# Where a fused kernel's weight conversions stand, and when its P tiles are loaded

## The chip, the core and the metric

The kernel runs on one core of a Trainium2 chip. The time is that of the device, in microseconds (us), from one launch to its end; three runs of the kernel before had a median of 1813.38 us (1813.12 to 1814.7). The engines are PE (TensorE, matmuls), PEld (its weight loads), DVE (VectorE), ACT (ScalarE), POOL (GpSimd) and SP (SyncE, which here issues every DMA in the order of the program).

## The reference, cut to what matters

```python
a = exp(phi - max(phi, axis=2)); a = a / (sum(a, axis=2) + 1e-09)          # 8 batches, 8 heads, 576 x 32
k_m = einsum('bhsm,bhsd->bhmd', a, k); v_m = einsum('bhsm,bhsd->bhmd', a, v)
attn = softmax(scale * q @ k_m.T)                                          # over 32 memory slots
x = (attn @ v_m), heads side by side: 4608 tokens x 512
h = x @ w_in;  x = (h - tanh(h)) @ w_out                                   # first layer, 512 -> 2048 -> 512
h = x @ w3;    out = where(h > 0, h, exp(min(h, 0)) - 1) @ w4              # second layer, the same sizes
```

The four weight matrices arrive as 64-bit floats. A value is used as a pair of words, high part and rest, and each product of pairs takes three matmuls.

## The kernel before, in words

**First layer.** The product `attn @ v_m @ w_in` is regrouped: `v_m @ w_in` (`vw_half`, L304, tile `vw_ps`, kept as `vw`) is made once for a pair of batches, and the softmax rows P (tile `p`, written to `p_dram` by the attention and loaded by `load_p`, L291) are multiplied with it (`h_unit`, L319, tile `h_ps`). The feed-forward width of 2048 is cut in four, the tokens in 16 tiles of 288, which makes 64 *blocks* (`bi` 0 to 63). A block is two *halves* (`i` 0 and 1), and a half does, in this order: one `h_unit`; the elementwise function of it (`g_a` to `g_d`: ACT L330 to L333, POOL L338, DVE L339, then DVE L344 and L345, and in the next half ACT L351 and POOL L352, tile `g`); two `x_unit` (L364, tile `x_ps`, the product with `w_out`), of which ACT copies the first (L371) and, after block 22, DVE the second (L373). `x_unit`, `vw_half` and parts of the attention share three PSUM buffers (`misc`). Every fourth block (3, 7, ..., 59) also makes the next group's `vw`, two `vw_half` in each of its halves; this is called a *border* below.

**Work on the side.** Two `Staged` queues of generators advance by one step each time `round()` is called: `units` with the 16 attention units (blocks 0 to 22; in each, DVE L120 makes a row maximum `cmax`, which PE transposes in the next round, L123), and `cv` with the weight conversions. A conversion of 128 x 512 weights loads `raw` (one of three buffers), waits some rounds, and then does one stage a round: ACT L48 (`abs`, into the one PSUM buffer `cv_m`), DVE L50 and L51, DVE L54 and L55 (which read `cv_m` for the last time and write `cv_a`), ACT L58, POOL L60. First-layer weights stay in SBUF; second-layer weights are staged in `wst` and stored to `w_dram` (L541). `cv` advances once a half, twice in blocks 0 to 6 and 28 and 29, and starts a conversion every second round. `need(kind, pg)` calls `round()` at once, as often as it takes until these weights are there, and `open_l2` at block 60 calls `drain()`, which does so until nothing is left; it then opens the second layer's pools where the first one's buffers were.

**Second layer.** From the end of block 63 on, PE goes through 18 token tiles of 256 with matmuls L420 and L457. Blocks 60 to 63 already load its first activations (`xr`, L393, summed by DVE L402) and weights.

Of the kernel before, what the change touches and what calls it, by code (L numbers as in the profile page):

```python
# [62 lines left out]
class Attention:  # L63
# [44 lines left out]
    def unit(self, u, nxt, eng, first_p=None):  # L108

        nc, wk, sm = self.nc, self.wk, self.sm  # L110
        b, g = divmod(u, 2)
# [8 lines left out]
        nc.vector.tensor_reduce(cmax, ph.rearrange("p h c m -> p h m c"), axis=AX.X, op=ALU.max)  # L120
        yield
        mT = ps_tile([128, 96], "mT")
        nc.tensor.transpose(mT, cmax.rearrange("p h m -> p (h m)"), ident[:96, :96])  # L123
# [116 lines left out]
class Staged:  # L240


    def __init__(self, gens=(), every=1):
        self.todo, self.live, self.every, self.wait = deque(gens), [], every, 0
        self.timed, self.rounds = deque(), 0
        self.first = deque()

    def at(self, rnd, gen):
        self.timed.append((rnd, gen))

    def round(self):
        while self.timed and self.timed[0][0] <= self.rounds:
            self.live.append(self.timed.popleft()[1])
        self.rounds += 1
        if self.wait > 0:
            self.wait -= 1
        if self.wait <= 0 and (self.first or self.todo):
            self.live.append((self.first or self.todo).popleft())
            self.wait = self.every
        for g in list(self.live):  # L260
            try:
                next(g)
            except StopIteration:
                self.live.remove(g)
# [6 lines left out]
class Moe1:  # L271


    def __init__(self, tc, ctx, const, p_dram, x2_dram):
        self.tc, self.nc, self.const = tc, tc.nc, const
        self.p_dram, self.x2_dram = p_dram, x2_dram
        pool = lambda name, n, **kw: ctx.enter_context(tc.tile_pool(name=name, bufs=n, reuse_waits="tile", **kw))
        self.x_p = pool("x2", 3)
        self.g_p = pool("g", 5)
        self.gw, self.gw1 = pool("gw", 3), pool("gw1", 1)  # L280
        self.p_p = pool("p", 2)
        self.vw_p = pool("vw", 1)
        self.vw, self.p, self.g, self.x2, self.work, self.x2_pool = {}, {}, {}, {}, {}, {}
# [195 lines left out]
def moe_kernel(tc, q, k, v, phi, w1, w2, w3, w4, out):  # L479
    nc = tc.nc  # L480
    with ExitStack() as top, tc.manual_schedule():
# [11 lines left out]
        m1 = Moe1(tc, l1a, const, p_dram, x2_dram)  # L493
# [18 lines left out]
        def conv(layer, kind, pg, c, lead=2):  # L512
# [6 lines left out]
            else:  # L519
                r0 = 256 * pg + 128 * c  # L520
                nc.sync.dma_start(out=raw, in_=w[r0:r0 + 128, :])
            for _ in range(lead + 1):
                yield
            staged = []
# [19 lines left out]
        conv_l1 = lambda kind, *pgs: [g for pg in pgs for g in conv_pair(1, kind, pg)]  # L544
# [15 lines left out]
        cv = Staged([conv(1, "i", 1, 1)] + conv_l1("o", 0, 1), 2)  # L560
        cv.wait = 4
        for k, g in enumerate(cv_first):
# [54 lines left out]
        def store_late():  # L617
            while late:
                m1.store_x(*late.pop(0))
# [49 lines left out]

        soon = deque()  # L670
        for bi, (ss, bp, sub, j) in enumerate(blocks):
# [28 lines left out]
            if at1_open and 2 * B - 1 in p_done:  # L700
# [3 lines left out]
                cv.first.extend(conv_l1("o", 4, 5))  # L704
            if bi == 18:
                cv.todo.extend(conv_l2)
            if bi == 24:
                cv.first.extend(conv_l1("i", 4, 5))
            if bi == 28:
# [3 lines left out]
            if nxt and nxt not in m1.p:  # L713
                m1.load_p(*nxt)
            for i in range(2):
                pg = 2 * sw + i
                m1.h_unit(sw, n, pg)
                m1.g_a(n, pg)
                m1.g_b(n, pg)
                store_late()  # L720
                if soon:
# [15 lines left out]
                m1.g_c(n, pg)  # L737
                if bi < 7 or 28 <= bi < 30:
                    cv.round()
                units.round()  # L740
                if vw_next:
# [59 lines left out]
```

## Time and profile before

| | |
|---|---|
| median of three runs | 1813.38 us |
| the profiled execution | 1815.06 us, span 1813.3 us, 1.8 us around it |
| PE busy | 1624.8 us, 90% of the span |
| PE busy, 0 to 100 us | 42.5 of 100 us |
| PE busy, 100 to 950 us | 729.5 of 850 us (sum over windows of 50 us) |
| DVE, ACT, POOL busy | 1215.8, 960.8, 755.3 us |
| mean granted TensorE clock | 0.956 of full speed |

The span has three stretches: the start with the first attention units (to about 72 us, where the first `h_unit` stands), the 64 blocks of the first layer (to 986 us), and the second layer, in which PE has no idle time to speak of. A time in a row is counted from the first instruction of the span. The end of the idle time before a row stands in brackets with what released it.

### The profile page before, as it was taken

Reading aid. Unit: us, or ns where it says so; the run is one execution under the profiler, and the core shown is the slowest. Engines: PE = TensorE matmul, PEld = TensorE weight load, DVE = VectorE, ACT = ScalarE, POOL = GpSimd, SP = SyncE. Lnnn points to the kernel's source line nnn. Section 1 sums busy time; section 2 is a strip of 40 time slices with the busy share of each in tenths; the row PEclk is TensorE's granted clock in tenths of the full one; section 3 lists DMA queues with packets and bytes.
Section 4 is the critical chain, followed back from the end, with each engine's and each line's share of the span. In section 5 each row is a group of like instructions: output and inputs, shape, how many; then the busy total and the mean of one; then the engine's idle time right before and its main releaser. Section 6 shows DMA issues by size and latency. Waiting matters only on the chain.

```text
span 1813.3 us, 30112 instructions
## 1 busy us (share of the span) xinstructions
PE 1624.8 (90%) x11496; PEld 1496.5 (83%) x11496; DVE 1215.8 (67%) x1805; ACT 960.8 (53%) x1713; POOL 755.3 (42%) x539
## 2 busy tenths in 40 slices
PE   4467879888888989999949999999999999999998
PEld 2356778888887989999949999999999999999997
DVE  6868777677877888788855555555555555555554
ACT  3456767677877878787845333333333333333332
POOL 3245645555655656665634222222222222222222
PEclk7678999899998989999979999999999999999999
DMA  9466565675545456666657721221221221211110
GB/s 241 133 165 177 150 185 171 168 200 165 191 163 167 155 165 196 204 198 200 199 163 263 300 59 59 59 59 59 59 59 59 59 59 59 59 59 59 59 35 24
DMA packets 140935, 238.40 MB, mean 131 GB/s; under 512 B 8184, under 2 KB 102392, under 8 KB 138744
## 3 DMA queue, kind: packets, MB, share of 16 engines
q1 hardware_dynamic: 140792, 236.49, 42.9%
q8 instruction: 91, 1.49, 0.4%
q14 instruction: 52, 0.43, 0.1%
HBM read 159.78 MB, written 75.50 MB: 130 GB/s over the span
## 4 chain that ended last, share of the span: by engine, by line
PE 68%; DVE 11%; ACT 7%; DMA 7%; issue 4%; POOL 2%; SPq 0%; DVEq 0%; ACTq 0%; POOLq 0%
PE h_ps L420 23%; PE o_ps L457 22%; PE x_ps L364 14%; PE h_ps L319 7%; DMA p<-p_dram 5%; DVE vw L309 2%; ACT vw L307 1%; DVE cv_a L55 1%; DVE cv_m L54 1%; DVE h_ps L339 1%; ACT t L330 1%; PE vw_ps L304 1%; ACT g L351 1%; DVE s L344 1%; ACT u L331 1%
## 5 line engine op out<-in xcount | busy, mean ns | idle before, releaser
L364 PE MATMUL x_ps<-g,w 128*128 128x288 f32 x3072 | 466.2, 305 | 69.0 <-DVE vw L309 27.9
L364 PEld LDWEIGHTS x_ps<-g,w 128*128 128x128 f32 x3072 | 433.6, 195 | 84.5 <-issue 23.9
L420 PEld LDWEIGHTS h_ps<-x,wi 128*128 128x128 f32 x3456 | 429.7, 190 | 11.7
L420 PE MATMUL h_ps<-x,wi 128*128 128x256 f32 x3456 | 433.2, 281 | 0.0
L446 POOL TENSOR_TENSOR e<-hm,e 128x512 fp32r<-128x512 f32 x144 | 186.9, 1298 | 588.1 <-ACT e L445 443.8
L457 PE MATMUL o_ps<-wo,e 128*128 128x512 f32 x1728 | 423.8, 394 | 0.7 <-POOL e L446 0.7
L457 PEld LDWEIGHTS o_ps<-wo,e 128*128 128x128 f32 x1728 | 314.8, 188 | 65.0 <-POOL e L446 1.1
L431 ACT ACTIVATE t_ps<-hm 128x512 f32<-128x512 f32 x144 | 86.7, 602 | 515.2 <-DVE hm L430 515.2
L338 POOL TENSOR_TENSOR v<-t,u 128x576 f32<-128x576 f32 x128 | 183.5, 1433 | 215.7 <-ACT u L331 153.9
L319 PE MATMUL h_ps<-p,vw 128*128 128x288 f32 x1536 | 242.5, 310 | 23.8 <-DMA p<-p_dram 21.4
L352 POOL TENSOR_TENSOR g<-s,g 128x576 fp32r<-128x576 f32 x128 | 191.7, 1498 | 146.1 <-ACT g L351 130.7
L319 PEld LDWEIGHTS h_ps<-p,vw 128*128 128x128 f32 x1536 | 223.6, 200 | 27.6 <-issue 15.4
L437 DVE SCALAR_TENSOR_TENSOR hm<-hm,t_ps 128x512 f32<-128x512 f32 x144 | 99.1, 688 | 200.5 <-ACT hm L432 200.5
L430 DVE TENSOR_SCALAR hm<-h_ps 128x512 f32<-128x512 f32 x144 | 99.6, 692 | 140.0 <-PE h_ps L420 140.0
L339 DVE TENSOR_TENSOR h_ps<-h_ps,t 128x576 f32<-128x576 f32 x128 | 98.0, 766 | 82.4 <-ACT u L331 80.8
L330 ACT ACTIVATE t<-h_ps 128x576 f32<-128x576 f32 x128 | 83.2, 650 | 96.9 <-issue 44.4
L309 DVE TENSOR_TENSOR vw<-vw_ps,vw 64x512 fp32r<-64x512 f32 x128 | 88.1, 689 | 66.7 <-ACT vw L307 64.7
L344 DVE SCALAR_TENSOR_TENSOR s<-s,v 128x576 f32<-128x576 f32 x128 | 114.4, 894 | 4.0 <-POOL v L338 3.9
L345 DVE COPY_PREDICATED s<-big,h_ps 128x576 f32<-128x576 uint32 x128 | 106.6, 833 | 10.7
L333 ACT ACTIVATE big<-u,bias 128x576 f32<-128x576 f32 x128 | 97.9, 765 | 10.9 <-DVE s L345 10.9
L439 DVE TENSOR_TENSOR hm<-hm,h_ps 128x512 f32<-128x512 f32 x144 | 98.9, 687 | 5.0
L438 DVE SCALAR_TENSOR_TENSOR hm<-hm,t_ps 128x512 f32<-128x512 f32 x144 | 98.9, 687 | 4.9
(86 smaller groups left out, 1744.2 us busy)
## 6 DMA issues: line engine op xcount, KB each, us to landing
x_dram<-x SPq DMA_DIRECT2D x128, 288.0 KB
xr<-x_dram SPq DMA_DIRECT2D x72, 512.0 KB
p<-p_dram SPq DMA_DIRECT2D x62, 576.0 KB
raw<-in_moe_w_in_dram SPq DMA_DIRECT2D x32, 512.0 KB
raw<-in_moe_w_out_dram SPq DMA_DIRECT2D x32, 512.0 KB
w_dram<-wst SPq DMA_DIRECT2D x32, 512.0 KB
kv<-in_k_dram SPq DMA_DIRECT2D x16, 576.0 KB
kv<-in_v_dram SPq DMA_DIRECT2D x16, 576.0 KB
```

Source lines behind the costliest of these rows:

```text
L309: nc.vector.tensor_tensor(lo, src, r32(hi), op=ALU.subtract)
L319: nc.tensor.matmul(ps[:, j, :NB], lhsT=vw[a][:, kc, 128 * j:128 * j + 128], rhs=p[:, kc, b, :], start=(k == 0), stop=(k == 5))
L330: nc.scalar.activation(t, w[0], ACTF.Tanh)
L338: nc.gpsimd.tensor_tensor(v, t, u, op=ALU.mult)
L339: nc.vector.tensor_tensor(h, h, t, op=ALU.subtract)
L344: nc.vector.scalar_tensor_tensor(s, s, G_B, v, op0=ALU.add, op1=ALU.mult)
L345: nc.vector.copy_predicated(s, big.bitcast(U32), d)
L352: nc.gpsimd.tensor_tensor(g[:, 1], s, r32(g[:, 0]), op=ALU.subtract)
L364: nc.tensor.matmul(ps, lhsT=wo[pg][:, a, j, 128 * dm:128 * dm + 128], rhs=g[:, b, j, :], start=(k == 0), stop=(k == 11))
L420: nc.tensor.matmul(ps[:, j], lhsT=w3[:, a, kc, 128 * j:128 * j + 128], rhs=x[:, b, kc, :], start=(k == 0), stop=(k == 11))
L446: nc.gpsimd.tensor_tensor(e[:, 1], hm, r32(e[:, 0]), op=ALU.subtract)
L457: nc.tensor.matmul(self.acc[n][tg], lhsT=e[:, a, j, 128 * tg:128 * tg + 128], rhs=w4[:, b, j, :], start=(pg == 0 and j == 0 and i == 0), s ...
```

## The change

It alters the first layer alone: when steps of the side queues are issued, and two pool sizes. No operation is added or removed in the computation.

- `Staged` gets a list `apart` and a method `half()`. A conversion's last yield before its `abs` is true, which puts it on that list, so that its next step (`abs`) is issued at the next `half()`: after `g_c` in the same half of a block, and not at the next `round()`.
- `cv` advances twice a half in blocks 26 to 29 (before 28 and 29). The second-layer conversions are queued at block 14 (before 18), and those of `w_in` parts 4 and 5 are put ahead of `w_out` parts 4 and 5.
- The pool of `p` has three buffers (before two), that of `g` four (before five). `load_p` for block `bi + 2` is issued in block `bi` after the second `h_unit`, if the attention units that it needs were done before this block; otherwise one block ahead at its top, as before.
- An attention unit from the fifth on waits one more round between `cmax` and its transposition; the first start of `cv.todo` is one round later.

```diff
@@ Attention.unit
         yield
+        if u >= 4:
+            yield
         mT = ps_tile([128, 96], "mT")
@@ Staged
-        self.first = deque()
+        self.first, self.apart = deque(), []
     def round(self):
+        self.half()
...
-        for g in list(self.live):
+        self.step([g for g in self.live if g not in self.apart])
+
+    def half(self):
+
+        gens, self.apart = self.apart, []
+        self.step(gens)
+
+    def step(self, gens):
+        for g in gens:
             try:
-                next(g)
+                if next(g):
+                    self.apart.append(g)
@@ Moe1
-        self.g_p = pool("g", 5)
+        self.g_p = pool("g", 4)
-        self.p_p = pool("p", 2)
+        self.p_p = pool("p", 3)
@@ conv
-            for _ in range(lead + 1):
-                yield
+            for k in range(lead + 1):
+                yield k == lead
@@ the blocks
-        cv.wait = 4
+        cv.wait = 5
-            if bi == 18:
+            if bi == 14:
                 cv.todo.extend(conv_l2)
             if bi == 24:
-                cv.first.extend(conv_l1("i", 4, 5))
+                cv.first.extendleft(reversed(conv_l1("i", 4, 5)))
...
+            p_there |= p_done
...
+                if i == 1 and bi + 2 < len(blocks):
+                    ass, abp, asub, aj = blocks[bi + 2]
+                    far = (2 * ass + asub, 4 * abp + aj)
+                    if all(u in p_there for u in range(2 * (far[1] // 2) + 2)):
+                        m1.load_p(*far)
...
                 m1.g_c(n, pg)
-                if bi < 7 or 28 <= bi < 30:
+                cv.half()
+                if bi < 7 or 26 <= bi < 30:
                     cv.round()
+                    cv.half()
```

The line numbers grow by up to 20 with it (L48 to L60 stay; L307 is L319 afterwards, L330 is L342, L371 is L383, L120 stays, L291 is L303, L379 is L391, L393 is L405, L541 is L553).

**At a border.** These are ACT's instructions in the two halves of border block 51, from the first half's `vw` copies on. Before:

```order
L307 ACTIVATE vw<-vw_ps 64x512 x4
L330 ACTIVATE t<-h_ps 128x576
L331 ACTIVATE u<-h_ps 128x576
L332 ACTIVATE s<-u,bias 128x576
L333 ACTIVATE big<-u,bias 128x576
L371 ACTIVATE x<-x_ps 128x288
L48 ACTIVATE cv_m<-raw 128x512
L351 ACTIVATE g<-s 128x576
L307 ACTIVATE vw<-vw_ps 64x512 x4
```

Now:

```order
L319 ACTIVATE vw<-vw_ps 64x512 x2
L48 ACTIVATE cv_m<-raw 128x512
L319 ACTIVATE vw<-vw_ps 64x512 x2
L342 ACTIVATE t<-h_ps 128x576
L343 ACTIVATE u<-h_ps 128x576
L344 ACTIVATE s<-u,bias 128x576
L345 ACTIVATE big<-u,bias 128x576
L383 ACTIVATE x<-x_ps 128x288
L58 ACTIVATE wst<-cv_a 128x512
L363 ACTIVATE g<-s 128x576
L319 ACTIVATE vw<-vw_ps 64x512 x4
```

The `abs` (L48) has moved from between the second half's copy of `x_ps` and its `vw` to the first half, between the two pairs of `vw` copies; L58, which before stood ahead of the first half's `vw`, stands where L48 stood.

**At block 60.** DVE between the last `vw` of border block 59 and the first sum of the second layer's activations. Before, of 16 rows of conversions in a row the first eight:

```order
L309 TENSOR_TENSOR vw<-vw_ps,vw 64x512 x2
L50 TENSOR_SCALAR cv_m<-cv_m 128x512
L51 TENSOR_SCALAR cv_m<-cv_m 128x512
L54 SCALAR_TENSOR_TENSOR cv_m<-raw,cv_m 128x512
L55 SCALAR_TENSOR_TENSOR cv_a<-raw,cv_m 128x512
L50 TENSOR_SCALAR cv_m<-cv_m 128x512
L51 TENSOR_SCALAR cv_m<-cv_m 128x512
L54 SCALAR_TENSOR_TENSOR cv_m<-raw,cv_m 128x512
L55 SCALAR_TENSOR_TENSOR cv_a<-raw,cv_m 128x512
```

Now:

```order
L321 TENSOR_TENSOR vw<-vw_ps,vw 64x512 x2
L351 TENSOR_TENSOR h_ps<-h_ps,t 128x2x288
L385 COPY x<-x_ps 128x288
L356 SCALAR_TENSOR_TENSOR s<-s,v 128x576
L357 COPY_PREDICATED s<-big,h_ps 128x576
L351 TENSOR_TENSOR h_ps<-h_ps,t 128x2x288
```

No DVE step of a conversion is left there; what `drain()` still issues is one POOL L60 and its store.

**SP's queue in the same place**, from a store of weights on. Before:

```order
L541 DMA w_dram<-wst 256x1x512 x4
L291 DMA p<-p_dram 128x1x1152
L379 DMA x_dram<-x 128x2x288
L393 DMA xr<-x_dram 128x4x256
L379 DMA x_dram<-x 128x2x288
L393 DMA xr<-x_dram 128x4x256
L291 DMA p<-p_dram 128x1x1152
L379 DMA x_dram<-x 128x2x288
L393 DMA xr<-x_dram 128x4x256 x2
L379 DMA x_dram<-x 128x2x288
```

Now:

```order
L553 DMA w_dram<-wst 256x1x512 x2
L391 DMA x_dram<-x 128x2x288
L405 DMA xr<-x_dram 128x4x256
L303 DMA p<-p_dram 128x1x1152
L391 DMA x_dram<-x 128x2x288
L405 DMA xr<-x_dram 128x4x256
L391 DMA x_dram<-x 128x2x288
L405 DMA xr<-x_dram 128x4x256 x2
L303 DMA p<-p_dram 128x1x1152
L391 DMA x_dram<-x 128x2x288
```

Of the loads of `p`, that of block 61 now stands before the stores; the one of block 62 stands behind one `xr` load, and that of block 63 behind all four.

## Rows read from the trace of the kernel before

**Rows 1.** Timeline of PE, steady blocks to a border: start, us, instruction [idle before]

```profile
711.80 1.77 PE L319 MATMUL h_ps<-p,vw 128*128 128x288 f32 x12
716.60 1.77 PE L319 MATMUL h_ps<-p,vw 128*128 128x288 f32 x12
722.82 1.78 PE L319 MATMUL h_ps<-p,vw 128*128 128x288 f32 x12
730.63 1.77 PE L319 MATMUL h_ps<-p,vw 128*128 128x288 f32 x12
...
739.29 1.78 PE L319 MATMUL h_ps<-p,vw 128*128 128x288 f32 x12
```

**Rows 2.** The same timeline one border earlier, its third half

```profile
685.44 1.78 PE L319 MATMUL h_ps<-p,vw 128*128 128x288 f32 x12
692.60 1.77 PE L319 MATMUL h_ps<-p,vw 128*128 128x288 f32 x12
```

**Rows 3.** Windows: start:end, length, busy (count) PE, PEld, DVE, ACT, POOL, clock, DMA share

```profile
666.00:915.00 249.00, 231.63 (x1700) 228.05 (x1700) 204.01 (x303) 202.80 (x347) 151.79 (x108) 0.99 0.62 197
...
734.50:739.30 4.80, 4.79 (x25) 4.80 (x26) 4.64 (x8) 3.84 (x7) 2.05 (x2) 0.64 0.39 142
```

**Rows 4.** Timeline of all engines, second half of the border at block 43

```profile
730.63 0.63 ACT L48 ACTIVATE cv_m<-raw 128x512 f32<-128x512 f32 x1 [2.46 <-DVE cv_a L55]
...
734.51 4.94 PE L364 MATMUL x_ps<-g,w 128*128 128x288 f32 x24 [2.12 <-DVE vw L309]
```

**Rows 5.** Timeline of PE, where `need` advances `cv` in block 37

```profile
647.87 1.77 PE L319 MATMUL h_ps<-p,vw 128*128 128x288 f32 x12
...
666.61 1.77 PE L319 MATMUL h_ps<-p,vw 128*128 128x288 f32 x12
```

**Rows 6.** Timeline of PE, blocks 60 to 63 and the second layer's first product

```profile
914.81 1.78 PE L319 MATMUL h_ps<-p,vw 128*128 128x288 f32 x12
...
939.04 2.29 PE L364 MATMUL x_ps<-g,w 128*128 128x288 f32 x8 [12.18 <-DVE x L373]
...
950.88 3.22 PE L319 MATMUL h_ps<-p,vw 128*128 128x288 f32 x12 [7.84 <-DMA p<-p_dram]
...
976.06 1.85 PE L319 MATMUL h_ps<-p,vw 128*128 128x288 f32 x12 [2.44 <-DMA p<-p_dram]
...
985.74 3.04 PE L420 MATMUL h_ps<-x,wi 128*128 128x256 f32 x24
```

**Rows 7.** Timeline of PE, first product of block 26 and of block 33

```profile
502.51 1.75 PE L319 MATMUL h_ps<-p,vw 128*128 128x288 f32 x12
597.96 1.74 PE L319 MATMUL h_ps<-p,vw 128*128 128x288 f32 x12
```

**Rows 8.** Timeline and windows in blocks 28 and 29, `cv` twice a half

```profile
538.03 1.58 DVE L344 SCALAR_TENSOR_TENSOR s<-s,v 128x576 f32<-128x576 f32 x1
...
546.02 0.75 DVE L344 SCALAR_TENSOR_TENSOR s<-s,v 128x576 f32<-128x576 f32 x1
...
543.65:550.81 7.16, 5.26 (x38) 4.83 (x37) 5.18 (x8) 4.57 (x8) 4.17 (x3) 1.00 0.66 232
```

**Rows 9.** Costliest groups: one of a conversion's four DVE passes: busy us, mean ns

```profile
L54 DVE SCALAR_TENSOR_TENSOR cv_m<-raw,cv_m 128x512 uint32<-128x512 uint32 x64 | 44.0, 687 | 0.2
```

**Rows 10.** Windows as above: blocks 14 to 18, no conversions

```profile
331.80:412.18 80.38, 70.16 (x627) 64.53 (x626) 58.59 (x93) 55.27 (x111) 42.66 (x30) 0.96 0.66 187
```

**Rows 11.** Waits of PE from 130 to 412 us: total us, times, longest

```profile
PE mT L123 <- DVE cmax L120: 6.9, 4, 2.9
PE h_ps L319 <- DMA p<-p_dram: 6.4, 2, 5.2
```

**Rows 12.** Chain of work that ended last: start, us, what

```profile
499.62 14.40 DMA p<-p_dram
```

**Rows 13.** Timeline, a steady block's `raw` load and ACT's `abs`

```profile
745.82 0.56 SPq L521 DMA_DIRECT2D raw<-in_moe_w_out_dram  x1
763.69 0.64 ACT L48 ACTIVATE cv_m<-raw 128x512 f32<-128x512 f32 x1 [0.37 <-DVE cv_a L55]
```

More of the change, by code (lines that the diff above doesn't have):

```diff
@@ L668, in step2 @@
                 m2.o_unit(*seq[idx - LAG2])
-        soon = deque()
+        soon, p_there = deque(), set()
         for bi, (ss, bp, sub, j) in enumerate(blocks):
```

## The prediction

> **What bounds the kernel now.** I read the windows first. In blocks 38 to 59 PE is busy 231.6 of 249 us [rows 3]; DVE and ACT have 45 us of idle time there and POOL more, so PE sets the pace and only a hole in PE can be won back. The timeline of PE then gives the price of each hole, if one takes the start of every half's first product. A steady half takes 716.60 - 711.80 = 4.80 us [rows 1]: 36 matmuls, no gap. Whatever is longer than that is a hole or extra matmuls. Over all 128 halves the excess lies in five places.
>
> (a) *Borders.* Three halves in a row take 6.22, 7.81 and 8.66 us [rows 1]. The `vw` matmuls take 1.42 us in each of the first two (6.22 - 4.80, a half without any stall), so the second half stalls for 1.59 us and the third for 3.86. The third one's cause stands in the rows of all engines: ACT sits for 2.46 us at `abs`, which may not overwrite `cv_m` before DVE has read it (L55); `vw`'s copies queue behind it, DVE's after them, and PE waits 2.12 us for the PSUM buffer [rows 4]. The granted clock is 0.64 of full speed in the stretch behind this [rows 3]. At the border before, the third half takes 7.16 us [rows 2]. Seven borders lie in blocks 35 to 59, four like the one and three like the other.
>
> (b) *Block 37.* Here `need` pushes four conversion rounds in a row between two products. The two halves from there take 666.61 - 647.87 = 18.74 us [rows 5].
>
> (c) *Blocks 60 to 63.* From block 60's first product to the second layer's first product 985.74 - 914.81 = 70.93 us pass [rows 6], against eight halves at 4.80 = 38.4. PE waits 12.18 us while `drain` runs four conversions through DVE one after another, and then 7.84 and 2.44 us for `p`, which was issued late.
>
> (d) *Blocks 26 to 32* take 597.96 - 502.51 = 95.45 us [rows 7]. In the halves with two rounds of `cv` it is a ring that takes 7.16 us, though DVE is busy for 5.18, ACT for 4.57 and PE for 5.26 of it [rows 8]: `abs` waits for DVE's L55, the next function's tanh stands behind `abs`, and DVE waits for that.
>
> (e) *The attention blocks.* From 130 to 412 us PE waits 6.9 us for `cmax` and 6.4 us for `p` [rows 11].
>
> **The change, part by part**, against the profiled execution's 1815.06 us (1.7 above the median; the forecast is made from the profiled one, as the difference is inside 0.1%).
>
> *T1, blocks 60 to 63: -18 us.* Since second-layer conversions begin at block 14 and the stall in block 37 is gone, the last `abs` is issued in block 58, and DVE has no conversion left at block 60. The hole of 12.18 us goes, the `p` of block 61 is issued ahead of the last stores, and with it the 7.84 us. Of the excess of 32.5 us, 3.8 is a border's third half (counted in T2), which leaves 28.7. I leave 11 of it standing: DVE still sums three `xr` tiles for the second layer, and SP still has the `xr` loads ahead of the `p` of blocks 62 and 63; the fourth waits for a sum, and blocks that pass in 9.6 us leave less time than a transfer of `p` took elsewhere, 14.40 us [rows 12]. Bounds: -26 (only the sums stay) to -8 (two late `p` of 7.84 us each and the sums).
>
> *T2, the borders behind block 33: -20 us.* `abs` stands in the first half now, where DVE's L55 has long run; in the second half ACT meets L58, whose input is a half old. I follow the rows: ACT's copy of `x_ps` ends 2.46 us ahead of `abs`, so `g` and `vw` come up to that much earlier, and the 2.12 us at PE vanish, as does the slow clock behind it. Third halves above 4.80: 4 x 2.36 + 3 x 3.86 = 21.0; second halves 7 x 1.59 = 11.1. I take 16 of the first, since `vw`'s second pair now waits for an `abs` of 0.64 us, and 4 of the second. Bounds: -30 (no stall stays) to -8 (the wait shrinks to what is left when `abs` merely changes place).
>
> *T3, block 37: -9 us.* The first-layer weights are complete in block 36, so `need` does nothing: 18.74 - 9.60 = 9.1. Bounds -9 to -7.
>
> *T4, blocks 26 to 32: -8 us.* Now eight halves (before four) do a conversion each. `abs` comes after `g`, when DVE is through L55, so the ring opens and DVE becomes the limit: its 5.18 us [rows 8] and some gaps make 5.7 us a half, and a border's half is 3.0 us longer (7.81 - 4.80) [rows 1], as in block 27. 6 x 5.7 + 2 x 8.7 + block 30 at 9.8, 31 at 15 and 32 at 10 = 86.4, against 95.45. Bounds: +8 (the ring only moves, and four more halves take 7.16) to -12. One row speaks against the low end: DVE's L344 takes 0.75 us alone and 1.58 us [rows 8] while POOL does L60. The Trainium skill (SBUF — State Buffer, "SBUF: two separate sides") has it that a DVE instruction with two SBUF inputs and a GpSimd instruction that reads SBUF exclude each other, and that the later one is blocked until the other ends; by that rule each conversion that meets an L344 costs up to a POOL instruction, and T4 would come out near zero. The two lengths of L344 agree with it. I keep -8, because half of the halves before had the same pairing.
>
> *T5, border 23 and its like: -3 us*, the stall of T2 once (2.1 and its slow clock); the earlier borders lie among attention work. Bounds 0 to -6.
>
> *T6, `p` in the attention blocks: -3 us.* Of the 6.4 us, 5.2 wait for a row that attention unit 7 stores just before [rows 11]; no third buffer helps there. I take the rest and two more like it later. Bounds 0 to -4. The fourth `g` buffer is waited for by ACT's `g`, which follows the copy of the very `x_unit` that frees it, and so costs nothing.
>
> *T7, the extra round of the attention: -6 us.* `cmax` is issued a round earlier than its transposition; the 6.9 us [rows 11] are what it can give. Bounds 0 to -12.
>
> *T8, four conversions in blocks 15 to 18: +4 us.* Each takes four DVE passes of 0.69 us [rows 9], together 11 us; in these blocks DVE is busy for 58.6 of 80.4 us [rows 10], and PE for 70.2. If DVE's idle time takes them, they are free; on the path they cost 11. I take a third, as DVE's chains hold the attention back. Bounds 0 to +11.
>
> Sum: -18 - 20 - 9 - 8 - 3 - 3 - 6 + 4 = -63, which gives **1752 us**. The start (to 72 us) I leave as it is: its conversions are bound by loads, +-3.
>
> **The rivals.** *Only the two holes close.* `abs` in another place may only move ACT's wait: the borders keep their length, because PE's wait is for `vw`, which ACT makes in four instructions either way. For it speaks that PE's 2.12 us begin with ACT's 2.46 but need not end with them; against it that nothing else is late in those rows [rows 4]. Then T1 (at -16) and T3 remain with the small ones set off by T8: 1815 - 16 - 9 = 1790.
>
> *Slower: `raw` lands too late.* `abs` is issued half a block sooner after its load. Before, 763.69 - 745.82 = 17.9 us lay between [rows 13]; now about 14 in a steady block, and 11.6 in blocks 26 to 29. If `raw` has not landed, ACT stops, and the function of every half behind it. The gain of 63 us is gone when 40 conversions each come later than the 1.6 us of slack that ACT has in a block, and eight later than 1.5: 40 x (L - 15.6) + 8 x (L - 13.1) = 63, so L = 16.5 us from issue to landing. At L = 17.5 the time is 1815 - 63 + 76 + 35 = 1863. A `p` of nearly the same size took 14.40 us [rows 12] at the worst of the late blocks, so this needs a transfer slower than those seen.
>
> *No change at all* would need the conversions to run out as late as before; the order of instructions excludes this.
>
> **How the numbers follow.** The forecast's own case has 0.81, the two holes alone 0.13, the slow case 0.04, and 0.02 falls within 0.2%, which is about what a measurement of this kernel can tell from no change (its three runs lie within 0.09%). The terms' bounds add up to -99 and -4 (T4 and T8 at their worst); that all lie at one end is unlikely, so the low end is 1722, the root of the squares (some 25 us) and a little more, and the high end 1790, where the second case stands. Faster 0.94, same 0.02, slower 0.04.
>
> **What would show it.** In the trace after: no half in blocks 36 to 38 above 5 us except the border's (T3); the third half of each border near 5 us and no wait of ACT's L48 for `cv_a` above 0.5 us there (T2); no four DVE passes in a row before the first sum of `xr`, and the second layer's first product 50 to 55 us after block 60's (T1); halves of 5.5 to 6 us in blocks 26 to 29 (T4); the waits of the transposition for `cmax` gone (T7). Wrong would be: ACT waiting for `raw` (the slow case), L344 near 1.6 us in every half of blocks 26 to 29, or PE waiting for `p` in blocks 62 and 63 longer than 11 us.

## The result and the profile after

The changed kernel takes 1770.76 us (median of 4 runs, 1769.16 to 1771.73), the kernel before 1814.04 us on the same chip: a ratio of 0.9756, with a 95% interval of 0.9737 to 0.9774. So 43 us are gone where 63 were forecast. The profiled execution after took 1771.73 us. The table cuts both executions at the same places, the start of a half's first product, as the prediction did.

| from | to | before, us | after, us | difference |
|---|---|---|---|---|
| start | block 0 | 72.27 | 77.00 | +4.7 |
| block 0 | block 4 | 94.30 | 100.11 | +5.8 |
| block 4 | block 10 | 103.77 | 102.27 | -1.5 |
| block 10 | block 14 | 61.46 | 66.14 | +4.7 |
| block 14 | block 19 | 80.38 | 84.74 | +4.4 |
| block 19 | block 23 | 53.43 | 57.65 | +4.2 |
| block 23 | block 26 | 36.90 | 33.26 | -3.6 |
| block 26 | block 33 | 95.45 | 83.01 | -12.4 |
| block 33 | block 37, second half | 49.91 | 47.39 | -2.5 |
| block 37, second half | block 38, second half | 18.74 | 9.60 | -9.1 |
| block 38, second half | block 60 | 248.20 | 232.11 | -16.1 |
| block 60 | second layer's first product | 70.93 | 49.80 | -21.1 |

Up to block 23 the changed kernel is 22 us slower; from there on it gains 65. (The lines of `kernel.py` moved: L319, L309, L364, L371 and L344 of before are L331, L321, L376, L383 and L356 now; L48 and L55 stayed.)

The timeline of PE at the border of block 43 answers to [rows 1]:

```profile
708.65 1.77 PE L331 MATMUL h_ps<-p,vw 128*128 128x288 f32 x12
714.87 1.78 PE L331 MATMUL h_ps<-p,vw 128*128 128x288 f32 x12
722.52 1.78 PE L331 MATMUL h_ps<-p,vw 128*128 128x288 f32 x12
727.33 1.77 PE L331 MATMUL h_ps<-p,vw 128*128 128x288 f32 x12
```

The three halves take 6.22, 7.65 and 4.81 us, where they took 6.22, 7.81 and 8.66. The third half's stall is gone, the second one's is not. The timeline of all engines in that second half answers to [rows 4] and says why:

```profile
715.04 0.62 ACT L48 ACTIVATE cv_m<-raw 128x512 f32<-128x512 f32 x1
715.17 1.39 DVE L321 TENSOR_TENSOR vw<-vw_ps,vw 64x512 fp32r<-64x512 f32 x2 [1.35 <-ACT vw L319]
...
720.15 1.82 PE L376 MATMUL x_ps<-g,w 128*128 128x288 f32 x12 [0.91 <-DVE vw L321]
```

ACT's `abs` (L48) starts without a wait (it had waited 2.46 us). PE still waits 0.91 us for DVE's part of `vw`, though no wait of `abs` stands ahead of it any more. What would shorten this wait was not tried.

Block 37 is two plain halves now, against the 18.74 us of [rows 5]:

```profile
651.57 1.77 PE L331 MATMUL h_ps<-p,vw 128*128 128x288 f32 x12
...
661.17 1.77 PE L331 MATMUL h_ps<-p,vw 128*128 128x288 f32 x12
```

From block 60 to the second layer (timelines of PE and DVE, against [rows 6]) neither the hole of 12.18 us nor a wait for `p` is left. One stall of 5.06 us stands instead: DVE's copy into `x` may not overwrite a tile whose store has not landed, and L357 is queued behind that copy:

```profile
893.28 1.78 PE L331 MATMUL h_ps<-p,vw 128*128 128x288 f32 x12
...
928.82 0.46 DVE L385 COPY x<-x_ps 128x288 f32<-128x288 f32 x1 [7.49 <-DMA x_dram<-x]
...
930.95 3.22 PE L331 MATMUL h_ps<-p,vw 128*128 128x288 f32 x12 [5.06 <-DVE s L357]
...
943.08 3.04 PE L432 MATMUL h_ps<-x,wi 128*128 128x256 f32 x24
```

Blocks 26 to 32 answer to [rows 7, 8]. The timelines, and the windows of blocks 28 to 30 and of the one bad half:

```profile
521.17 1.75 PE L331 MATMUL h_ps<-p,vw 128*128 128x288 f32 x12
...
536.90 1.78 PE L331 MATMUL h_ps<-p,vw 128*128 128x288 f32 x12
539.57 0.64 ACT L48 ACTIVATE cv_m<-raw 128x512 f32<-128x512 f32 x1 [1.93 <-DMA raw<-in_moe_w_in_dram]
545.00 3.25 PE L376 MATMUL x_ps<-g,w 128*128 128x288 f32 x12 [2.96 <-ACT x L383]
549.33 2.41 PE L331 MATMUL h_ps<-p,vw 128*128 128x288 f32 x12
554.74 1.75 PE L331 MATMUL h_ps<-p,vw 128*128 128x288 f32 x12
559.50 1.75 PE L331 MATMUL h_ps<-p,vw 128*128 128x288 f32 x12
...
569.02 1.75 PE L331 MATMUL h_ps<-p,vw 128*128 128x288 f32 x12
575.02 1.82 PE L331 MATMUL h_ps<-p,vw 128*128 128x288 f32 x12 [1.07 <-DVE s L357]
580.33 1.83 PE L331 MATMUL h_ps<-p,vw 128*128 128x288 f32 x12 [0.31 <-PE x_ps L376]
...
604.18 1.75 PE L331 MATMUL h_ps<-p,vw 128*128 128x288 f32 x12
```

```profile
550.00:564.00 14.00, 14.00 (x105) 14.00 (x104) 13.42 (x20) 12.04 (x22) 9.60 (x7) 0.97 0.59 204
...
543.00:550.00 7.00, 5.00 (x21) 5.00 (x22) 6.22 (x10) 5.10 (x10) 4.04 (x3) 0.57 0.54 185
```

Halves with a conversion pass in 4.76 us with PE never idle; the ring of 7.16 us is gone. In block 30 two halves take 6.00 and 5.31 us, and PE waits for DVE. One half, 536.90 to 549.33, takes 12.43: `abs` waits 1.93 us for its `raw`, the copy of `x` behind it comes late, PE waits 2.96 us, and from 543 to 550 us, in and behind PE's pause of 2.96 us, the granted clock is 0.57 of full speed, so mostly at the lower of its two levels (1.2 GHz).

Last, ACT's waits for `raw` between block 0 and block 4, where time was lost (total us, times, longest; in the kernel before it was one wait of 3.0 us):

```profile
ACT cv_m L48 <- DMA raw<-in_moe_w_in_dram: 12.3, 3, 8.2
```

### The profile page after: what moved, and what is told of

Same layout as the page of the kernel before. It is cut to its first block, busy times and chain, and to the rows that moved or that the text cites. A ratio compares the mean times of both kernels' runs of the same rounds, so it can differ in the third digit from the quotient of the medians.

```text
span 1770.0 us, 30078 instructions
## 1 busy us (share of the span) xinstructions
PE 1618.5 (91%) x11496; PEld 1494.5 (84%) x11496; DVE 1225.3 (69%) x1805; ACT 954.7 (54%) x1713; POOL 766.3 (43%) x539
## 4 chain that ended last, share of the span: by engine, by line
PE 70%; DMA 10%; DVE 7%; ACT 5%; issue 3%; POOL 2%; SPq 1%; DVEq 0%; POOLq 0%; ACTq 0%
PE h_ps L432 23%; PE o_ps L469 22%; PE x_ps L376 14%; PE h_ps L331 8%; DMA x_dram<-x 5%; DMA raw<-in_moe_w_in_dram 3%; PE vw_ps L316 2%; DVE s L356 1%; DVE vw L321 1%; DMA kv<-in_v_dram 1%; ACT t L342 1%; DMA xr<-x_dram 1%; DMA phi<-in_phi_dram 1%; ACT u L343 1%; ACT big L345 1%
## 5 line engine op out<-in xcount | busy, mean ns | idle before, releaser
L376 PE MATMUL x_ps<-g,w 128*128 128x288 f32 x3072 | 454.5, 301 | 30.4 <-DVE vw L321 9.6
L376 PEld LDWEIGHTS x_ps<-g,w 128*128 128x128 f32 x3072 | 427.2, 192 | 41.6 <-ACT x L383 11.0
L331 PE MATMUL h_ps<-p,vw 128*128 128x288 f32 x1536 | 241.8, 309 | 17.8 <-DVE s L357 6.1
L331 PEld LDWEIGHTS h_ps<-p,vw 128*128 128x128 f32 x1536 | 222.9, 199 | 20.9 <-issue 12.7
L364 POOL TENSOR_TENSOR g<-s,g 128x576 fp32r<-128x576 f32 x128 | 203.2, 1588 | 83.9 <-ACT g L363 81.3
L342 ACT ACTIVATE t<-h_ps 128x576 f32<-128x576 f32 x128 | 83.2, 650 | 82.2 <-PE h_ps L331 39.6
L356 DVE SCALAR_TENSOR_TENSOR s<-s,v 128x576 f32<-128x576 f32 x128 | 121.5, 949 | 1.8 <-POOL v L350 1.8
L321 DVE TENSOR_TENSOR vw<-vw_ps,vw 64x512 fp32r<-64x512 f32 x128 | 88.1, 688 | 40.4 <-ACT vw L319 38.4
L357 DVE COPY_PREDICATED s<-big,h_ps 128x576 f32<-128x576 uint32 x128 | 106.3, 831 | 11.3 <-DVE s L356 0.5
```

What stands on the lines that cost most here:

```text
L321: nc.vector.tensor_tensor(lo, src, r32(hi), op=ALU.subtract)
L331: nc.tensor.matmul(ps[:, j, :NB], lhsT=vw[a][:, kc, 128 * j:128 * j + 128], rhs=p[:, kc, b, :], start=(k == 0), stop=(k == 5))
L342: nc.scalar.activation(t, w[0], ACTF.Tanh)
L356: nc.vector.scalar_tensor_tensor(s, s, G_B, v, op0=ALU.add, op1=ALU.mult)
L357: nc.vector.copy_predicated(s, big.bitcast(U32), d)
L364: nc.gpsimd.tensor_tensor(g[:, 1], s, r32(g[:, 0]), op=ALU.subtract)
```

## The experiments

Twelve more kernels were measured beside the kernel before. Ratios are to the kernel before on the same chip; its own median was 1814 to 1819 us in the different groups, so a difference of a few microseconds between two medians below is better taken from the ratios. A control for single stretches: x_l2 (below) is the same program as the changed kernel up to block 14. It reached block 0 at 74.40 us and block 14 at 346.93, the changed kernel at 77.00 and 345.52. So 2.6 us of the "+4.7" at the start are scatter of an execution, and a difference of some 2 us in one stretch says nothing. The changed kernel and its variants with `abs` half a unit apart reach block 0 between 72.3 and 77.0 us, the kernel before at 72.27.

| kernel | median, us | ratio, 95% interval |
|---|---|---|
| changed | 1770.76 | 0.9756 [0.9737, 0.9774] |
| x_abs: changed, `abs` in the round again | 1820.00 | 1.0003 [0.9981, 1.0026] |
| y_babs: before, `abs` half a unit apart alone | 1778.70 | 0.9777 [0.9752, 0.9803] |
| z_mbuf: x_abs with P as before, `cv_m` in two SBUF buffers | 1836.24 | 1.0101 [1.0082, 1.0121] |
| z_m1: the same, one SBUF buffer | 1886.93 | 1.0376 [1.0354, 1.0398] |
| x_l2: changed, second layer from block 18 | 1783.33 | 0.9822 [0.9795, 0.9849] |
| x_round: changed without the extra round | 1762.94 | 0.9698 [0.9676, 0.9720] |
| z_start: changed, units a round earlier | 1761.99 | 0.9686 [0.9666, 0.9707] |
| y_round8: extra round from unit 8 on | 1767.02 | 0.9716 [0.9690, 0.9743] |
| x_p: changed, P one block ahead | 1769.07 | 0.9738 [0.9716, 0.9760] |
| y_plate: P early from block 22 on | 1761.88 | 0.9682 [0.9654, 0.9709] |
| y_best: the parts that paid | 1752.65 | 0.9634 [0.9606, 0.9661] |
| z_best: y_best and z_start | 1751.94 | 0.9641 [0.9621, 0.9662] |

### The place of `abs`: x_abs and y_babs

x_abs takes the half step out of the changed kernel:

```diff
-            for k in range(lead + 1):
-                yield k == lead
+            for k in range(lead + 1):
+                yield
```

> The changed kernel (1770.8 us), but abs is issued in the round again, as before; all else stays. Theory of the forecast (T2, T4): the place of abs alone makes the stalls at the borders and the ring of the halves with a conversion each. The third halves of the borders behind block 33 go from 4.80 back to 7.2 or 8.7 us (+16 to +21 in all), halves of blocks 26 to 29 to 5.7 to 7.2 us (+8 to +15), the halves behind block 60 stay: 1795 to 1807 us. Rival (the two holes alone, or the third P buffer and the fewer g buffers close the borders): the third halves stay at 4.80 and the time within 4 us of 1771.

It took 1820.0 us, more than the theory's 1795 to 1807, and as long as the kernel before. The timeline at its border of block 43:

```profile
756.38 1.78 PE L331 MATMUL h_ps<-p,vw 128*128 128x288 f32 x12
756.38 0.63 ACT L48 ACTIVATE cv_m<-raw 128x512 f32<-128x512 f32 x1 [2.46 <-DVE cv_a L55]
760.27 3.44 PE L376 MATMUL x_ps<-g,w 128*128 128x288 f32 x24 [2.11 <-DVE vw L321]
763.54 1.77 PE L331 MATMUL h_ps<-p,vw 128*128 128x288 f32 x12
```

These are the 2.46 us at ACT and the 2.1 us at PE of [rows 4] again, with the third half at 7.16 us. P's third buffer and the early load stand in this kernel too, so they do not close the border. Against the changed kernel the stretches give +15.7 us in blocks 38 to 59, +20 in blocks 26 to 32, +5 in blocks 23 to 25. Block 37 (11.35 us) keeps 7.4 of its gain of 9.1 us, and the stretch from block 60 nearly all of its own.

y_babs is the other way round, the kernel before with the half step alone (`Staged` and the first start of the queue are as in the changed kernel; those lines are left out here):

```diff
-            for _ in range(lead + 1):
-                yield
+            for k in range(lead + 1):
+                yield k == lead
...
                 m1.g_c(n, pg)
+                cv.half()
                 if bi < 7 or 28 <= bi < 30:
                     cv.round()
+                    cv.half()
```

> The kernel before with abs's place alone (the half step, and the start's queue one round later, as in the changed kernel); rates, order, the attention's round and P's buffers as before. Theory (what x_abs took back in single stretches, weighed one by one): blocks 26 to 32 lose the ring (-8 to -14), the borders behind block 33 their third half (-19 to -22), blocks 0 to 25 gain 0 to 7; block 37 stays at 18.7 us and the drain at block 60 too: 1777 to 1788 us. Rival: the 49 us between x_abs and the changed kernel belong to abs's place whatever the rest: 1766 us. Second rival: without the earlier load P comes late in the faster blocks 38 to 59 and takes most of it back: 1795 us or more.

1778.7 us, inside the theory's range. Its blocks 26 to 32 take 80.64 us (before 95.45), the stretch from the second half of block 38 to block 60 takes 234.8 (before 248.2), while block 37 and the drain stay near their old length (16.96 and 69.2 us). So the half step alone is worth 2.2%, about 40 us. All other edits together bring the remaining 3 or 4 us, and as the two intervals overlap, even these are not sure. They do not do nothing: what they gain in block 37 (7.4 us) and from block 60 on (19.4) they lose up to block 23, which y_babs reaches at 462.52 us and the changed kernel at 487.91. The second rival is out: the third halves are near 4.8 us without an early P, and only a little of it is left (2.7 us more than the changed kernel in blocks 38 to 59).

### What the place of `abs` takes away: z_mbuf and z_m1

That the wait, and not the order on ACT, is what costs can be tried by leaving `abs` where it was and giving `cv_m` a second buffer. So that PSUM's other tiles stay as they are, `cv_m` moves to SBUF; z_m1 is the same with one buffer, so that the two differ in the wait alone. Both load P one block ahead, with two buffers.

```diff
-    m = psum.tile(list(w_hi.shape), F32, tag="c", name="cv_m")
+    m = pool.tile(list(w_hi.shape), F32, tag="m", name="cv_m")          # z_mbuf: two buffers
+    m = pool.tile(list(w_hi.shape), F32, tag="m", bufs=1, name="cv_m")  # z_m1
```

> x_abs (abs in the round again, 1820 us), with cv_m in two SBUF buffers where it had one of PSUM; to make room, P has two buffers and no earlier load. Theory (T2, T4): what costs at the borders and in the ring is abs's wait for the one cv_m, in whichever place; with a second one ACT doesn't wait for L55, third halves are near 4.8 us (some with a wait for P, 1 to 2 us) and blocks 26 to 32 take 83 to 87 us: 1775 to 1787 us. Rival: it is abs's place among g and the copies on ACT, or the four passes on DVE, that cost; then the second buffer changes nothing: 1815 to 1825 us. Third: the DVE passes on two SBUF inputs (L54, L55) and POOL's L60 shut each other out, all conversions get longer: above 1825.

> The same with cv_m in one SBUF buffer: the wait of abs for L55 is there again, and only the memory differs from x_abs. Theory: third halves of 7.2 to 8.7 us and the ring return, 1813 to 1825 us, some 40 us above the two buffers. Rival: cv_m in SBUF is what helps (its passes are shorter there); then within 5 us of the two buffers.

The two differ by 50.7 us (the theory said some 40), but both lie higher than it said: z_mbuf is 16 us above x_abs, on the third theory's side. The groups of instructions show both effects. ACT's group in z_m1 and then in z_mbuf (busy us, mean ns, idle us before, and what ended it):

```profile
L48 ACT ACTIVATE cv_m<-raw 128x512 f32<-128x512 f32 x64 | 42.9, 670 | 191.2 <-DVE cv_a L55 176.7 <-DMA raw<-in_moe_w_in_dram 14.5
```

```profile
L48 ACT ACTIVATE cv_m<-raw 128x512 f32<-128x512 f32 x64 | 42.6, 666 | 20.4 <-DMA raw<-in_moe_w_in_dram 20.4
```

The wait of `abs` for L55 goes from 176.7 us to nothing, and with it 50 us of the kernel. That is more than the wait costs in x_abs, where it is 94.1 us, since L55 itself is later here. At the border of block 43 the third half is 5.94 us with two buffers and 8.80 with one; the 4.8 that was expected is not reached. DVE's conversion passes, in x_abs, z_m1 and z_mbuf:

```profile
L55 DVE SCALAR_TENSOR_TENSOR cv_a<-raw,cv_m 128x512 uint32<-128x512 uint32 x64 | 44.0, 688 | 2.9
```

```profile
L55 DVE SCALAR_TENSOR_TENSOR cv_a<-raw,cv_m 128x512 uint32<-128x512 uint32 x64 | 83.6, 1307 | 2.9
```

```profile
L55 DVE SCALAR_TENSOR_TENSOR cv_a<-raw,cv_m 128x512 uint32<-128x512 uint32 x64 | 92.0, 1438 | 2.9
```

L55 is 688 ns each time with `cv_m` in PSUM and on the mean about twice that in SBUF. L54 goes from 687 ns to 1165 and 1136, and POOL's L60 from 1.3 us to 1.6. The four passes of all conversions keep DVE busy for 252 us in z_mbuf, against 177 in x_abs. This is why a second buffer there doesn't pay: what it saves in waits is more than eaten by the passes. The half step gets the first without the second.

### The second layer's conversions: x_l2

```diff
-            if bi == 14:
+            if bi == 18:
                 cv.todo.extend(conv_l2)
```

> The changed kernel, but the second layer's conversions begin at block 18 again. By the order of its instructions blocks 15 to 18 hold no conversion, and three conversions stand at block 60 again in a row. Theory (T1 and T8): 4 to 8 us less in blocks 14 to 22, and at block 60 DVE's hole of 12 us and a late p return, 15 to 20 us more: 1778 to 1787 us. Rival: with abs in another place and p loaded sooner the conversions at block 60 hide beside PE, so only the gain remains: 1763 to 1767 us.

1783.3 us, as the theory said. Blocks 14 to 18 take 79.64 us (changed 84.74, before 80.38), so four conversions cost 5.1 us there. At block 60 PE stands as in [rows 6]:

```profile
910.16 2.29 PE L376 MATMUL x_ps<-g,w 128*128 128x288 f32 x8 [11.78 <-DVE x L385]
```

From block 60 to the second layer's first product it takes 65.0 us (changed 49.80). The hole is the drain's, not P's.

### The extra round of the attention: x_round, y_round8, z_start

```diff
-        if u >= 4:
-            yield
```

> The changed kernel without the extra round between cmax and its transposition. Theory of the forecast (T7): the round saved the waits of the transposition for cmax; without it 6 us more in blocks 5 to 22, 1777 us. Rival: the extra round gave nothing, since it makes every unit of attention a half longer, and is part of why blocks 10 to 23 became 13 us longer; without it these lose 4 to 8 us: 1763 to 1767 us.

1762.9 us: the rival's answer. The place differs from the rival's, though. By block 4, x_round is 14.2 us ahead (162.93 against 177.11; 3.9 of them are there at block 0 already, which is within the scatter of the start), and from there to block 26 it is 3.3 us slower than the changed kernel (347.39 against 344.06). The queue of SP between block 0 and block 2 shows what happens; first the changed kernel:

```profile
113.06 0.68 SPq L303 DMA_DIRECT2D p<-p_dram  x1
113.80 0.42 SPq L530 DMA_DIRECT2D raw<-in_moe_w_in_dram  x1
114.31 0.84 SPq L98 DMA_DIRECT2D kv<-in_k_dram  x1
115.21 0.58 SPq L99 DMA_DIRECT2D kv<-in_v_dram  x1
115.83 4.71 SPq L303 DMA_DIRECT2D p<-p_dram  x1
120.58 4.31 SPq L530 DMA_DIRECT2D raw<-in_moe_w_in_dram  x1
...
128.81 0.64 ACT L48 ACTIVATE cv_m<-raw 128x512 f32<-128x512 f32 x1 [8.24 <-DMA raw<-in_moe_w_in_dram]
```

and then x_round:

```profile
101.99 0.40 SPq L98 DMA_DIRECT2D kv<-in_k_dram  x1
102.44 0.99 SPq L99 DMA_DIRECT2D kv<-in_v_dram  x1
105.01 0.68 SPq L301 DMA_DIRECT2D p<-p_dram  x1
105.75 0.42 SPq L528 DMA_DIRECT2D raw<-in_moe_w_in_dram  x1
...
121.40 0.65 ACT L48 ACTIVATE cv_m<-raw 128x512 f32<-128x512 f32 x1 [1.85 <-DMA raw<-in_moe_w_in_dram]
```

The round delays not only the transposition but all that a unit does behind it, its loads of the next k and v among it (576 KB each). They now stand behind the first P and `raw` and ahead of the second, the issues of P and `raw` take 4.71 and 4.31 us of SP's time, and ACT waits 8.24 us with the functions queued behind it. A long issue alone does not do it: in x_round SP spends 5.35 us on a store of `vm` at 112.08, but behind the second P and `raw`.

y_round8 keeps the round for units 8 and later (`if u >= 8`).

> The changed kernel, with the extra round of the attention for units 8 and later only. Theory: x_round's gain of 14 us up to block 4 comes from units 4 to 7, whose loads of k and v are pushed behind P and raw in SP's queue, and later units' extra round is worth 3 us: 1756 to 1760 us, less than the 1763 of x_round; block 37 pays up to 2 us for one late conversion. Rival: each unit pays for its round, wherever it stands, since the rows of P come later: 1765 to 1768 us, between the changed kernel and x_round.

1767.0 us, the rival's range, yet its stretches speak for the theory up to block 26: reached at 507.79 us, 13.4 ahead of the changed kernel and 2.5 ahead of x_round. It loses most of this later, 4.5 us in blocks 26 and 27, 6.6 in block 37, where one conversion is late again, and 2.6 from there to block 60; behind block 60 it gains 3.7. My "up to 2 us" for block 37 was wrong; why blocks 26 and 27 got longer was not followed.

z_start separates "a unit is a round longer" from "what is behind the round comes later". It keeps the round and begins the units a round earlier:

```diff
-            units.at(22 + 7 * (u - 4), unit(u))
+            units.at(21 + 7 * (u - 4), unit(u))
```

> The changed kernel with the extra round, but units 4 and later begin one round earlier, so that everything behind the extra round stands where it stood before and only cmax is a round earlier. Theory: the round costs because it makes the rest of a unit, its loads of k and v and its store of P later; with the earlier start that is gone, and cmax's waits are saved: 1758 to 1763 us. Rival: the cost is of a unit being longer (its tiles are held a round more, and its neighbours wait): 1768 to 1773 us, as the changed kernel.

1762.0 us, the theory's. k and v are issued at 103.89 and 104.34 us again, and block 4 is reached at 163.48. So the length of the unit costs nothing; the delay of what stands behind the round does. It isn't faster than x_round either (1762.94): that `cmax` is issued a round earlier brings nothing that can be measured.

### The early load of P: x_p and y_plate

x_p restores two P buffers, five for `g`, and the load one block ahead. y_plate keeps the changed pools and asks `22 <= bi` for the load two blocks ahead.

> The changed kernel, but P is loaded one block ahead only, with two P buffers and five for g, as before. Theory: the earlier load stands ahead of raw in SP's queue in blocks 1 to 4 and makes ACT wait (8.2 us in one place after), and it costs PE at blocks 0 to 2; taking it away gives back 6 to 10 us up to block 4, and costs 5 to 10 us again where PE waited for p (blocks 24 to 29, 61 to 63): 1765 to 1775 us, with the shift between the stretches. Rival: the longer start comes from the later first round of the queue and abs's place, not from p; then up to block 4 nothing moves (within 2 us) and the end loses 5 to 10: 1776 to 1781 us.

> The changed kernel, but P is loaded two blocks ahead only from block 22 on; buffers as in the changed kernel. Theory: the earlier load is what lengthens blocks 2 to 3 (6 us) and 19 to 22 (4 us), and is worth 5 us in blocks 38 to 59 and 5 in 24 to 29: 1760 to 1764 us. Rival: the four g buffers lengthen the blocks of the attention (x_p had five again), or the difference there is the usual scatter of loads: 1769 to 1772 us.

x_p is 1769.1 us, as the theory said in total, but not for the reason that I gave: ACT still waits 8.0 us for `raw` near 125 us, so that wait is the extra round's. Up to block 26 x_p gains 9.2 us all the same (511.93 against 521.17; 3.1 of them at block 0, within the scatter). Behind it, it loses: in blocks 38 to 59 PE waits for P again (waits of PE, 654 to 892 us), and the stretch is 5.1 us longer.

```profile
PE h_ps L331 <- DMA p<-p_dram: 3.0, 3, 1.6
```

y_plate has both, 1761.9 us: 5.7 us ahead at block 26 (1.5 at block 0) and no loss behind. In blocks 10 to 13 the rows show the mechanism. Waits of ACT, the changed kernel from 279 to 346 us and y_plate from 279 to 341:

```profile
ACT x L383 <- DMA x_dram<-x: 16.4, 4, 5.8
```

```profile
ACT x L383 <- DMA x_dram<-x: 5.8, 1, 5.8
```

The early P stands in SP's queue ahead of the stores of `x`; ACT's copy waits for its tile until the store has landed. The other kernels agree. The six with an early P in these blocks (changed, x_abs, x_l2, x_round, z_start, y_round8) take 65.3 to 69.5 us there, and ACT waits 11.4 to 16.9 us for stores of `x`; those without (before, y_babs, x_p, y_plate, y_best, z_best) take 59.4 to 62.8 us and wait 5.8 to 8.8. The four buffers of `g` are not it, as y_plate has four as well. The rest of the balance is less clear. In blocks 4 to 9 x_p and y_plate are 4 us slower than the changed kernel (106.7 and 106.4 against 102.3), though y_best is not (103.5). In blocks 19 to 22, where y_plate gains 2.4 us, the waits for stores are alike (5.5 and 5.1 us), and the cause there stays open. ACT's waits for `raw` up to block 4 do not go with the early P: 14.4 us in the changed kernel, 13.6 in y_plate, 11.3 in x_p.

### The parts that paid: y_best and z_best

y_best is the changed kernel without the extra round, with `22 <= bi` for the early P, and

```diff
-            if bi == 14:
+            if bi == 16:
                 cv.todo.extend(conv_l2)
...
-                if bi < 7 or 26 <= bi < 30:
+                if bi < 7 or 26 <= bi < 32:
```

> The changed kernel without the extra round, with P two blocks ahead from block 22 only, the second layer's conversions from block 16 and two rounds a half in blocks 26 to 31. Theory: 8 us from the round, 4 from P in blocks 19 to 22, 2.5 from two conversions fewer in blocks 15 to 18, 0 to 2 back in blocks 30 and 31: 1754 to 1758 us. Rival: the three meet in the same slack of blocks 0 to 22 and do not add up: 1761 to 1764 us.

> y_best (1752.7 us) with the extra round and units 4 and later one round earlier. Theory: 0 to 3 us less than y_best from cmax's waits, 1749 to 1753 us. Rival: as the changed kernel's round, 4 to 8 us more: 1757 to 1761 us.

1752.65 us, below the expected 1754, and with a ratio of 0.9634 [0.9606, 0.9661] clearly faster than the changed kernel's 0.9756 [0.9737, 0.9774]. The three do add up: block 23 is reached at 462.53 us, where the kernel before needs 465.61 and the changed one 487.91. The two rounds a half in blocks 30 and 31 cost more than the 0 to 2 us expected: blocks 30 to 32 take 39.1 us against 35.2. z_best is the same within its interval: the extra round, even well placed, is worth nothing.

## Why the prediction was right, and where not

The time fell in the forecast's range. By itself it does not decide for the forecast: at 1771 us it lies 19 us above the 1752 forecast and 19 below the 1790 of the rival with the two holes. What decides is where the time went. Term by term, forecast and measured (profiled executions):

- **T1, blocks 60 to 63: -18, measured -17.3.** 70.93 - 49.80 = 21.1, less 3.8 for the third half of a border that was counted in T2. Right in its mechanism: x_l2 brings the hole back. What stays standing is not only the sums of `xr`, but 5.06 us for a store of `x`.
- **T2, the borders: -20, measured -22.3.** All seven third halves are at 4.80 or 4.81, which is 20.9 of their 21.0; of the second halves' 11.1 only 1.4 is gone (0.13 to 0.18 us each, 0.43 in block 47), where I took 4. In the half behind the third one `abs` still waits 1.2 us for L55 (at 729.14, for one), and PE does not stop for it. The cause is shown by x_abs, y_babs and the pair z_m1 and z_mbuf: the wait of `abs` for the one `cv_m`.
- **T3, block 37: -9, measured -9.1.**
- **T4, blocks 26 to 32: -8, measured -12.4.** (The prediction's own sum, 86.4 against 95.45, gives -9.) Right in what becomes the limit, wrong in when PE meets it: no half of PE is at 5.5 to 6 us in blocks 26 to 29, but DVE's own round is. Its copies into `x` (L385) start at 555.13, 560.64, 566.79, 572.13 and 578.17 us, 5.3 to 6.2 apart, while PE's halves start 4.76 apart. So DVE falls behind, and PE first waits for it in block 30, whose halves take 6.00 and 5.31. In x_p the halves from the second one of block 28 to the end of block 30 take 5.3 to 6.1 us, 5.7 on the mean, as T4 had it. Without the half step the ring comes back as the bound of +8 said: 103.0 us in x_abs against 95.45 before.
- **T5, border 23: -3, measured -3.6** (blocks 23 to 25).
- **T6, T7 and T8, and the start: -5, measured +22.3** (block 23 reached at 487.91 instead of 465.61). This is 27 us worse than forecast and more than the whole miss of 20; T2, T4 and T5 came out 7 us better and hid a part of it. Up to block 23, x_round gives back 10.9 us, y_plate 5.7 and x_l2 3.3, together 20 of the 22. T8 was right (+4 forecast, +5.1 in blocks 14 to 18 by x_l2).
- **The step that failed is T7**, "`cmax` is issued a round earlier than its transposition; the 6.9 us [rows 11] are what it can give". The waits did go, but the prediction did not count what else is moved by a `yield` in the middle of a generator: the loads of k and v behind it. Without the round the kernel is 7.8 us faster by the medians and 10 by the ratios. The loss falls in blocks 0 to 3, for which the sum had no term. The start before them, which the prediction left at +-3, came out at +4.7, and that is within its scatter.
- **T6 failed too**, with "no third buffer helps there. I take the rest". The early load was priced by the waits for P alone. It costs some 6 us up to block 26 (5.7 by the stretches of y_plate), since it stands ahead of the stores of `x` in the one queue; blocks 10 to 13 alone are 4.5 us longer than in y_plate. Behind block 23 it is worth some 11 us: from there to the second layer x_p takes 463.5 us and y_plate 452.8. The prediction had no term for that.
- **The range's low end** was worked out loosely: the root of the squares is 25 us for the distances to the upper bounds, but 16 for those to the lower ones.

Of the rivals, *only the two holes close* is out: the borders shrank, and x_abs, which has both holes closed, is no faster than the kernel before. *`raw` lands too late* is not the case behind block 33, where ACT never waits for `raw`; it does happen in one half of block 27 (1.93 us) and in blocks 0 to 3 (12.3 us), so the danger was seen rightly, and lay for the most part in other blocks than those that were priced. It was not tried how much later `raw` could come.

DVE's L356, whose two lengths stood behind the doubt about T4, still has both (timeline of DVE, blocks 29 and 30):

```profile
561.01 1.55 DVE L356 SCALAR_TENSOR_TENSOR s<-s,v 128x576 f32<-128x576 f32 x1
...
567.16 0.75 DVE L356 SCALAR_TENSOR_TENSOR s<-s,v 128x576 f32<-128x576 f32 x1
...
572.50 1.47 DVE L356 SCALAR_TENSOR_TENSOR s<-s,v 128x576 f32<-128x576 f32 x1
```

The long ones start while POOL's L364 runs (560.50 to 561.95 us and 571.91 to 573.36), the short one as it ends (567.19). DVE's round is 6.15 and 6.04 us with the two long ones and 5.34 with the short one. In block 29 PE is never idle, so the long one costs nothing at once; but it adds to DVE's lag, and in block 30 the L357 that PE waits 1.07 us for stands right behind the one of 1.47 us. The Trainium skill (SBUF — State Buffer, "SBUF: two separate sides") says that a DVE instruction with two SBUF inputs and a GpSimd instruction that reads SBUF exclude each other; the trace agrees, most plainly in z_mbuf and z_m1, where L54 and L55 become such instructions and L55 takes 1438 and 1307 ns on the mean instead of 688. That the rule would bring T4 near zero did not come true.

## What to carry to other kernels

An instruction that waits for a single buffer can be moved to where its buffer has long been free, and need not stand where its turn comes: here the half step was worth 40 us without one instruction less. A round added to a generator, or a load issued sooner, moves everything behind it in the shared DMA queue; list those transfers with their sizes before pricing the wait that is to go. Here the buffer for prefetch paid behind block 23, where two halves pass in 9.6 us and a load of P was seen to take 14.40 [rows 12], and cost time in the attention blocks, where stores of `x` stood behind it; a condition on the block kept the gain alone.

## What the runs showed of the hardware

In the changed kernel, with `cv_m` in PSUM, all 64 of L55 take 0.69 us, whatever POOL does. With both inputs in SBUF, in z_mbuf, 17 of the 64 take 0.69 us and the other 47 take 1.56 to 1.81. Rows of DVE and POOL in z_mbuf:

```profile
732.90 0.68 DVE L54 SCALAR_TENSOR_TENSOR cv_m<-raw,cv_m 128x512 uint32<-128x512 uint32 x1
732.93 1.81 POOL L60 TENSOR_TENSOR wst<-cv_a,wst 128x512 fp32r<-128x512 f32 x1
733.62 1.67 DVE L55 SCALAR_TENSOR_TENSOR cv_a<-raw,cv_m 128x512 uint32<-128x512 uint32 x1
...
738.68 0.41 DVE L50 TENSOR_SCALAR cv_m<-cv_m 128x512 f32<-128x512 f32 x1
```

L54 starts before POOL's L60 and takes 0.68 us; L55 starts while L60 runs and takes 1.67, ending 0.55 us after it (735.29 against 734.74). L60 is longer too, 1.81 us against 1.3 in the changed kernel. A pass that reads and writes `cv_m` alone, L50, takes 0.67 to 0.71 us each time with `cv_m` in PSUM. In SBUF it can be shorter, but not each time: in z_mbuf 46 of the 64 take 0.40 to 0.43 us and the others 0.63 to 1.87; in z_m1 17 take 0.40 to 0.45 and the others 0.74 to 1.60, and the mean, 1.02 us, is above that of PSUM. So SBUF is the faster place for this pass only at its best, and PSUM the better one for the kernel.

Issues on SP are not free when much is under way: behind k and v (576 KB each) the issues of P and `raw` took 4.71 and 4.31 us, where those ahead of k and v had taken 0.68 and 0.42.
